# A state-space convolution beside a mixture of experts: totals of scales by way of DRAM, the first block's operands kept, and three changes of order

## The chip, the cores and the metric

The kernel runs on one core of a Trainium2 chip. The time is the device time of one execution in microseconds (us), given as the median of the runs. The core's engines run their own instruction streams in order and wait for each other by semaphores: TensorE (PE in the profile, its weight loads PEld), VectorE (DVE), ScalarE (ACT), GpSimd (POOL) and SyncE (SP). DMAs are issued from SP and POOL in the kernel before.

## The reference, cut to what matters

```python
xn = layernorm(A_u)                              # 2048 tokens, 512 wide
# A: a diagonal state-space kernel K per channel, and a causal convolution
P  = exp(dt * A * l)                             # 512 channels, 128 states, 2048 steps, complex
K  = einsum("dn,dnl,dn->dl", C, P, dt * B).real
y  = irfft(rfft(pad(xn.T)) * rfft(pad(K))) + xn * Dskip
# B: eight experts, all of them chosen for every token
gates = softmax(xn @ w_gate)                     # top 8 of 8
for e in range(8):
    out += gates[:, e] * (silu(xn @ w1[e]) @ w2[e])   # w1 512x1792, w2 1792x512
return x + y + out
```

## The kernel before, in words

**Precision.** Every large product is made from float16 pairs: a float32 operand is scaled by a power of two and split into a high half (ACT: `hilo`'s activation, L442) and a low half (DVE: L445), and a product is three matmuls, high by high, high by low, low by high. The scale of a weight matrix comes from its sum of squares: ACT squares pieces and accumulates per partition (`square`, L438), DVE adds the columns (`prepass_end`, L406), and the total over the 128 partitions is a matmul of a matrix of ones with that one column (`pow2_total`, L160 to L171: the matmul at L170 into a PSUM tile, a copy out by ACT at L165). `pow2_scale` then makes the power of two on DVE. There is such a total for each of `w1[e]` and `w2[e]` (tot_w; expert 0's `w1` has tot_a and tot_b instead), and one for each of the 32 chunks of the state-space part (tot_k).

**Blocks.** Tokens go in four blocks of 512 (tb), and the loops are expert e, block tb, then four groups d of the 1792 hidden columns (seven pairs pr of 256: 2, 2, 2, 1). In every block but the very first, the first product is a Strassen-like scheme of seven half-size products (`block`, `product`, L1307): it needs seven sums and differences of quarters of x in `xop`, and seven of quarters of `w1` in `w1s`. Each group has four slots: products into three PSUM banks A, B, C (tiles hb), with copies of A into B (L1526) and B into C (L1534) and copies out (`keep`, L1521: scC, sE, scB) on ACT. POOL adds sE to scC and scB by accumulating DMAs (L1492); ACT then applies silu (L1323) and makes the high half of the hidden values (L1327: ahl), DVE the low half (L1336). The second product pops finished units of it from a list (`pop`, L1290 to L1292: tiles y, 512 columns). A block's y is scaled by the gate on ACT (`evacuate`, L1266: ye) and accumulated in DRAM.

**Operands of x.** The seven forms of a block's x, high and low, lie in DRAM (`xd`), and the seven slices of `xop` are loaded again for every block (L1517), each in the last group of the block before, as soon as its product is issued. They are made once, during expert 0: `x_sums` normalises two tiles of tokens on DVE and makes the sums, `x_high` (L250) and `x_low` (L257) split them, and `x_turn` transposes them on TensorE (L274, tiles tp), after which ACT copies them out (L285) and SP sends them. The very first block (e = 0, tb = 0) is worked plainly (`plain`, L1572) from `xT0`, all four tiles of x normalised (`xplain`, L296 and L298), split (L304), transposed (`xplain_turn`, L308) and copied into `xT0` (`xplain_out`: tiles 0, 1, 3 by ACT at L315, tile 2 by DVE at L313). `xT0` is not kept: for the seven other experts block 0 is loaded, normalised and transposed a second time, in eight turns, as the last of the blocks.

**The state-space part (s4)** runs in the background beside the experts, 32 chunks of 16 channels: tables on DVE, the kernel K by small matmuls (L729, tile kgen), squares and a copy out by ACT (`s4_kernel_out`: row krow, tile ksb at L737 and L738), a change of layout by way of DRAM (kd at L743, four loads of kt at L745), a scale (`s4_ksplit`: the total tot_k, then `s4_kscale`, `s4_khigh`, `s4_klow`), transforms by matmul (uf, kf, yp) and the convolution itself on DVE (L831, L832).

**What sets the order.** The order of the instructions on each engine is written by hand. A clock counts slots (four per group; the first block has 14). `side`, `mid` and `early` hold work for given slots of expert 0 (`at`, `put`). `work` is a list of items (squares, splits, the ends of a prepass) from which `work_on` takes up to two per slot; `bg_run` lets the s4 generators run as far as a budget of DVE time goes. tp, tot, kgen, uf, kf, yp and the gates' logits share one PSUM bank: `take_bank` hands it on, and a holder that still has to be read is read first (`bank_free`, `bank_wait`).

```python
        st = pow2_total(r, 1, f"w{e}_{w}")        # prepass_end, L408
        yield
        if bank["out"]:
            take_bank()
```

**The start.** `first_square`, `first_split` and `keep_busy` stand in a hand-written row from L1094 on: squares of the first weight pieces, the first scale sA from two of them, fillers on TensorE (L1105), and the splits of the first two pieces. `third` queues the split of the third piece.

**The end.** The last block's four output tiles are made by DVE straight from PSUM onto the loaded sum (L1273), and SP stores each (L1275).

Of the kernel before, what the change touches and what calls it, by code (L numbers as in the profile page):

```python
# [32 lines left out]
def s4_moe_kernel(  # L33
# [59 lines left out]
    xnd = dr.tile([P, NT, D], F32, name="xnd")  # L93
    kds = [dr.tile([P, 4, 64], F32, name=f"kd{n}") for n in range(2)]
# [5 lines left out]
             "act": 0.0, "act0": 0.0, "pe1": 0.0, "actleft": 0.0}  # L100
# [10 lines left out]
    def bank_free():  # L111

        if bank["out"]:
            take_bank()
        return clock["slot"] > bank["at"]
# [56 lines left out]

    def pow2_scale(dst, st, nm, add=0):

        it = sb.tile([P, st.shape[-1]], I32, tag="p2b", name=f"it_{nm}", bufs=2)
        V.tensor_scalar(it, st.bitcast(I32), 24, 23, op0=ALU.logical_shift_right, op1=ALU.logical_shift_left)
        V.tensor_scalar(dst.bitcast(I32), it, -1.0, float((204 + add) << 23), op0=ALU.mult, op1=ALU.add)
# [41 lines left out]
    def x_stats(g):  # L219
        if g:  # L220
            xs_["rs8", g] = norm_stats(g)
        else:
            rs8 = xs_["rs8", 0] = sb.tile([P, TPB], F32, tag="rs8", name="rs8again")
            V.tensor_scalar(rs8, rstd[:, 0:TPB], float(2 ** XSH), None, op0=ALU.mult)
# [65 lines left out]

    xp = {}

    def xplain(j, rs8):

        xn = sb.tile([P, D], F32, tag="fa", name=f"xn{j}")
# [14 lines left out]
    def xplain_out(j):  # L310
        dst = xT0.rearrange("p a k t -> p (a k) t")[:, :, j * P:(j + 1) * P]
        if j == 2:
            V.tensor_copy(dst, xp[j])  # L313
        else:
            S.copy(dst, xp[j])  # L315
# [88 lines left out]
    def prepass_end(e, w, n):  # L404
# [3 lines left out]
        st = pow2_total(r, 1, f"w{e}_{w}")  # L408
        yield
        if bank["out"]:  # L410
            take_bank()
# [46 lines left out]
    def w1_split(e, pr, raw):  # L458

        dst = w1s[pr].rearrange("p a o c -> p a (o c)")  # L460
# [6 lines left out]
    def w2_split(e, pr, raw):  # L467
        return hilo(w2s[pr].rearrange("p a f d -> p a (f d)"), raw.rearrange("p a c -> p (a c)"), scales[e][:, 1:2])
# [30 lines left out]
    def piece_end(e, w, n, ready):  # L499
        st = {}  # L500

        def s0(raw):
            st["g"] = prepass_end(e, w, n)
            step(0)
            clock["dve"] += 0.2

        def step(n):
            st["at"] = now()
            next(st["g"], None)
            done.add((e, w, n))  # L510

        def s1(raw):
            step(1)

        def s2(raw):
            step(2)
            clock["dve"] += 2.5

        def later():
            return now() > st["at"] + 1 and bank_free() and now() + 1 not in turns  # L520
        its = [Item(None, [s0], ready), Item(None, [s1], later), Item(None, [s2], later)]
        for it in its:
            it.e, it.w = e, w
        return its
# [27 lines left out]
    def work_on(limit):  # L552
        while limit > 0:
# [18 lines left out]
            limit -= 1  # L572
            last = not it.steps
# [160 lines left out]
    def s4_kernel_out(c):  # L734
# [8 lines left out]
        nc.sync.dma_start(kd, ksb.rearrange("p j g m -> p j (g m)"))  # L743
        for jh in range(4):
            nc.sync.dma_start(kt[32 * jh:32 * jh + 32].rearrange("x (s g) m -> x s (g m)", s=4),  # L745
                              kd[:, jh, :].rearrange("(s x) c -> x s c", s=4))
        s4["kt", c] = kt

# [216 lines left out]
    def s4_ksplit(c):  # L965

        yield from until(("ke", c))
        yield from bank_wait()
        s4["kst", c] = pow2_total(s4["krow", c], 1, f"k{c}", lambda: s4.update({("read", c): now()}))
        s4["total", c] = now()  # L970
        yield None
        while ("read", c) not in s4:
            bank_free()
            if ("read", c) not in s4:
                yield None
        yield from until(("read", c), more=0)
# [142 lines left out]
    sq(2)  # L1119
    stA = pow2_total(row2[:, 0:1], 1, "a")  # L1120
    take_bank()
    xplain_turn(1)
    keep_busy(8, ident)
# [3 lines left out]
    xplain_out(0)  # L1127
    xplain_turn(2)
    low0 = first_split(0)
    xplain(3, rs8_0)  # L1130
    keep_busy(8, ident)
    xplain_out(1)
    xplain_turn(3)
    xplain_out(2)
    low0()
    xplain_out(3)
    keep_busy(8, ident)
    sq(3)
    sq(4)
    low1 = first_split(1)  # L1140
    sq(5, True)
    sq(6)
    low1()
# [118 lines left out]
    def evacuate(e, i, y):  # L1262
# [9 lines left out]
        else:  # L1272
            V.scalar_tensor_tensor(stg[i], y, g, stg[i], op0=ALU.mult, op1=ALU.add)  # L1273
        if e == E - 1 and i >= NT - TPB:
            nc.sync.dma_start(out[i * P:(i + 1) * P, :], stg[i])  # L1275
# [90 lines left out]
    early, mid = {}, {}  # L1366
# [58 lines left out]
    halves = [(g, a) for g in (2, 3, 0) for a in range(2)]  # L1425
    for n, (g, a) in enumerate(halves):
        s0 = 20 + 4 * n
        at(s0, lambda g=g, a=a: x_high(g, a))
# [9 lines left out]
        if a == 0:  # L1438
            at(s0 + 3, lambda g=g: x_sums(g, 1))
            if g:  # L1440
                at(s0 + 3, lambda g=g: load_x((g + 1) % NB))
        elif g:
            if g + 1 < NB:
                at(s0 + 1, lambda g=g: norm_sums(g + 1))
            at(s0 + 2, lambda g=g: x_stats((g + 1) % NB))
            at(s0 + 3, lambda g=g: x_sums((g + 1) % NB, 0))

    def slot(e, tb, d, s, pops):
# [16 lines left out]
        elif e == 0 and tb == 1:  # L1465
            work_on(2 if d < 3 else 0)
# [27 lines left out]
    def block(e, tb, d):  # L1494
# [32 lines left out]
        clock["act"] += 2 * at_(n * TH)  # L1527
        if later:
            later.pop(0)()
# [31 lines left out]
    def plain():  # L1561

        for f in range(NF):
# [5 lines left out]
            for k in range(KT):  # L1569
                o = ((0, 1), (3, 2))[fh][k // 2]  # L1570
                for (a, b) in ((0, 0), (0, 1), (1, 0)):
                    T.matmul(h, w1s[pr][:, a, o, k % 2 * P:(k % 2 + 1) * P], xT0[:, b, k, :],  # L1572
                             start=(n == 0), stop=(n == 3 * KT - 1))
                    n += 1
# [5 lines left out]
            if f == 1:  # L1580
                activate(0, 0, 0, hb[0], 0, 0, True, high)
            activate(0, 0, pr, hb[f % 3], fh, 0, True, high)
            for g in high:
                g()
            if f == 1:
                third()
# [76 lines left out]
```

## Time and profile before

| what | value |
| --- | --- |
| median of 3 runs | 2345.7 us (2345.11 to 2345.76) |
| the profiled execution's own time | 2344.99 us |
| its span | 2343.2 us |
| TensorE busy | 2324.7 us, 17818 matmuls |
| DVE busy | 1964.2 us |
| ACT busy | 1473.5 us |
| POOL busy | 339.6 us |
| DMA moved | 319.68 MB |

Rows of the timeline read: start in us from the span's start, duration, engine, line of the kernel, operation, out<-in, shapes, count; in brackets how long the engine idled before and what ended that. Rows of groups end with busy time, the mean duration in ns, and the idle time before them. Several instructions in a row of one kind are merged into one row, with the count after x. A matmul's duration contains its way through the array, so matmuls of one stream overlap; the distance between two starts is what one costs the stream.

### The profile page before, as it was taken

Reading aid. Unit: us, or ns where it says so; the run is one execution under the profiler, and the core shown is the slowest. Engines: PE = TensorE matmul, PEld = TensorE weight load, DVE = VectorE, ACT = ScalarE, POOL = GpSimd, SP = SyncE. Lnnn points to the kernel's source line nnn. Section 1 sums busy time; section 2 is a strip of 40 time slices with the busy share of each in tenths; the row PEclk is TensorE's granted clock in tenths of the full one; section 3 lists DMA queues with packets and bytes.
Section 4 is the critical chain, followed back from the end, with each engine's and each line's share of the span. In section 5 each row is a group of like instructions: output and inputs, shape, how many; then the busy total and the mean of one; then the engine's idle time right before and its main releaser. Section 6 shows DMA issues by size and latency. Waiting matters only on the chain.

```text
span 2343.2 us, 45501 instructions
## 1 busy us (share of the span) xinstructions
PE 2324.7 (99%) x17818; PEld 1552.8 (66%) x17818; DVE 1964.2 (84%) x3814; ACT 1473.5 (63%) x2596; POOL 339.6 (14%) x394
## 2 busy tenths in 40 slices
PE   8999999999999999999999999999999999999999
PEld 4567666666666666666666666666666666666665
DVE  7864878889898899998899989998899988997721
ACT  7586667556665566665666657666576665765543
POOL 0011001121111211101111111111111110111112
PEclk9999999999999999999999999999999999999999
DMA  7586555774667746654556455565465654643456
GB/s 252 167 254 145 144 156 148 163 158 95 139 143 165 155 102 138 154 130 102 115 127 166 120 105 122 132 151 121 103 147 117 150 124 95 150 89 69 83 114 149
DMA packets 330503, 319.68 MB, mean 136 GB/s; under 512 B 190832, under 2 KB 223088, under 8 KB 329968
## 3 DMA queue, kind: packets, MB, share of 16 engines
q1 hardware_dynamic: 274416, 223.17, 32.4%
q0 software_dynamic: 55872, 93.61, 25.3%
q8 instruction: 139, 2.28, 0.4%
q14 instruction: 76, 0.62, 0.1%
HBM read 202.14 MB, written 65.01 MB: 114 GB/s over the span
## 4 chain that ended last, share of the span: by engine, by line
PE 94%; ACT 2%; issue 2%; DVE 1%; DMA 1%; SPq 0%; DVEq 0%; ACTq 0%; POOLq 0%
PE hb L1307 42%; PE y L1291 16%; PE y L1292 16%; PE y L1290 16%; PE kgen L729 1%; PE yp L860 1%; PE kf L800 1%; PE uf L787 1%; DMA scC<-sE 0%; PE tp L274 0%; ACT ahl L1327 0%; ACT fa L1323 0%; ACT w1s L442 0%; PE hb L1572 0%; DMA raw<-in_w_dram 0%
## 5 line engine op out<-in xcount | busy, mean ns | idle before, releaser
L1307 PE MATMUL hb<-xop,w1s 128*128 128x256 f16 x9114 | 1072.8, 273 | 3.3 <-ACT scC L1521 2.0
L1307 PEld LDWEIGHTS <-w1s 128*128 128x128 f16 x9114 | 889.0, 98 | 171.7 <-issue 5.1
L1290 PE MATMUL y<-w2s,ahl 128*128 128x512 f16 x1792 | 679.2, 379 | 0.9 <-ACT ye L1266 0.9
L1292 PE MATMUL y<-w2s,ahl 128*128 128x512 f16 x1792 | 679.2, 379 | 0.0
L1291 PE MATMUL y<-w2s,ahl 128*128 128x512 f16 x1792 | 679.2, 379 | 0.0
L1292 PEld LDWEIGHTS <-ahl 128*128 128x128 f16 x1792 | 175.3, 98 | 211.4
L1492 POOL DMA_DIRECT2D scC<-sE x124 | 117.6, 948 | 1295.0 <-ACT sE L1521 1095.0
L1323 ACT ACTIVATE fa<-hb,sc 128x512 f32<-128x512 f32 (+1 forms) x252 | 160.3, 636 | 199.4 <-PE hb L1307 198.9
L1291 PEld LDWEIGHTS <-ahl 128*128 128x128 f16 x1792 | 175.3, 98 | 162.2 <-issue 1.2
L832 DVE TENSOR_TENSOR s<-s,tm 128x720 f32<-128x720 f32 (+14 forms) x480 | 268.9, 560 | 16.6
L1290 PEld LDWEIGHTS <-ahl 128*128 128x128 f16 x1792 | 175.3, 98 | 161.1
L831 DVE TENSOR_TENSOR tm<-v,k 128x720 f32<-128x720 f32 (+14 forms) x480 | 267.3, 557 | 10.3
L1336 DVE SCALAR_TENSOR_TENSOR ahl<-fa,sc,ahl 128x512 f16<-128x512 f32 (+1 forms) x262 | 178.7, 682 | 57.6 <-ACT ahl L1327 57.3
L1534 ACT COPY hb<-hb 128x512 f32<-128x512 f32 x124 | 64.2, 518 | 240.5 <-PE hb L1307 240.3
L1327 ACT ACTIVATE ahl<-fa,sc 128x512 f16<-128x512 f32 (+1 forms) x262 | 175.8, 671 | 8.5
L1526 ACT COPY hb<-hb 128x512 f32<-128x512 f32 x124 | 64.3, 518 | 176.2 <-PE hb L1307 175.4
L1492 POOL DMA_DIRECT2D scB<-sE x124 | 107.5, 867 | 426.8 <-ACT scB L1521 287.6
L1336 DVE SCALAR_TENSOR_TENSOR ahl<-scB,sc,ahl 128x512 f16<-128x512 f32 x124 | 84.4, 681 | 77.4 <-ACT ahl L1327 74.1
L717 DVE TENSOR_TENSOR tb<-ta,tt 128x64 f32<-128x64 f32 (+2 forms) x192 | 132.0, 687 | 5.7
L711 DVE TENSOR_TENSOR ta<-tb,zr 128x64 f32<-128x64 f32 (+2 forms) x192 | 131.6, 686 | 5.3
L1269 POOL DMA_DIRECT2D oacc<-ye x108 | 95.9, 1339 | 252.8 <-ACT ye L1266 251.1
L714 DVE TENSOR_TENSOR tt<-tb,zi 128x64 f32<-128x64 f32 (+2 forms) x192 | 130.4, 679 | 0.0
(245 smaller groups left out, 2444.6 us busy)
## 6 DMA issues: line engine op xcount, KB each, us to landing
xop<-xd SPq DMA_DIRECT2D x210, 256.0 KB, 4.0
pp<-in_w_dram SPq DMA_DIRECT2D x98, 512.0 KB, 4.2
raw<-in_w_dram SPq DMA_DIRECT2D x56, 512.0 KB, 4.8
oacc<-ye POOLq DMA_DIRECT2D x108, 256.0 KB, 6.2
scC<-sE POOLq DMA_DIRECT2D x93, 256.0 KB, 4.2
scB<-sE POOLq DMA_DIRECT2D x93, 256.0 KB, 3.9
raw<-in_w_dram SPq DMA_DIRECT2D x52, 256.0 KB, 3.4
raw<-in_w_dram SPq DMA_DIRECT2D x104, 128.0 KB, 3.8
```

The source lines that it names most:

```text
L711: V.tensor_tensor(ta, tin, zrv, op=ALU.mult)
L717: V.tensor_tensor(tout, ta, tt, op=ALU.add)
L831: V.tensor_tensor(tm, v3f[:, :, 0:n], kb, op=ALU.mult)
L832: V.tensor_tensor(s3[:, :, m:], s3[:, :, m:], tm, op=ALU.add)
L1290: T.matmul(y, lhs[0], w2s[pr][:, 0, fh, :], start=(c == 0), stop=False)
L1291: T.matmul(y, lhs[0], w2s[pr][:, 1, fh, :], start=False, stop=False)
L1292: T.matmul(y, lhs[1], w2s[pr][:, 0, fh, :], start=False, stop=(c == NF - 1))
L1307: T.matmul(dst[:, q, :], w1s[pr][:, a, wo, k * P:(k + 1) * P], xop[:, xo, b, k, :], start=(first_mm and q == 0 and n == 0), stop=(n == 5), ...
L1323: S.activation(fa, src[:, :n], AF.Silu, scale=w1_unscale(e, d if whole else prs[0]))
L1327: S.activation(ahl[:, 0, :n], fa, AF.Copy, scale=scales[e][:, 3:4])
L1336: V.scalar_tensor_tensor(ahl[:, 1, :n], fa, sc[:, 3:4], ahl[:, 0, :n], op0=ALU.mult, op1=ALU.subtract)
L1492: nc.gpsimd.dma_start(dst, src, accum_op=ALU.add)
```

## The change

**Totals.** Three new helpers take the place of `pow2_total` for every expert but the first and for all s4 chunks: the column of 128 partial sums is stored to DRAM (`total_send`), loaded back so that each partition holds all 128 (`total_fetch`), and summed along the row by ACT (`total_sum`). In `prepass_end` the steps lie at least two slots apart; in the s4 part the column is sent just behind kd, fetched behind the kt loads, and summed two slots after the chunk's `s4_kernel_out`.

```diff
+    def total_send(row, nm):
+        rd = dr.tile([P, 1], F32, name=f"rd_{nm}")
+        nc.sync.dma_start(rd, row)
+        return rd
+    def total_fetch(rd, nm):
+        bt = sb.tile([P, P], F32, tag="bt", name=f"bt_{nm}", bufs=1)
+        nc.sync.dma_start(bt, rd.rearrange("p a -> (p a)").partition_broadcast(P))
+        return bt
+    def total_sum(bt, nm):
+        st = sb.tile([P, 1], F32, tag="p2a", name=f"st_{nm}", bufs=2)
+        S.activation(bt, bt, AF.Copy, accum_out=st)
+        clock["act"] += at_(P) + 0.2
+        return st
...
     def s4_ksplit(c):
         yield from until(("ke", c))
-        yield from bank_wait()
-        s4["kst", c] = pow2_total(s4["krow", c], 1, f"k{c}", lambda: s4.update({("read", c): now()}))
-        s4["total", c] = now()
+        s4["kst", c] = total_sum(s4["kbt", c], f"k{c}")
```

`piece_end` becomes one item of five steps instead of three items, and no longer asks for the bank. `bank_free` refuses the bank in a slot of which `work_on` took two items.

**Block 0's operands.** The normalised tiles of the start are kept (tag hh) and stored; the three of the seven forms that are plain quarters go from `xT0` to `xd[0]` in slots 8 to 10, and `xT0` as a whole to `x0d` in slot 11. In place of the second pass `xT0` is loaded again (slot 31), and the other four forms are made from what is already transposed.

```diff
+    def x0_send(n):
+        if n < 4:
+            nc.sync.dma_start(xnd[:, n, :], xp["xn", n])
+        elif n < 7:
+            k, t = ((0, 0), (2, 0), (2, TH))[n - 4]
+            for b in range(2):
+                nc.sync.dma_start(xd[0][:, n - 4, b], xT0[:, b, k:k + 2, t:t + TH])
+        else:
+            nc.sync.dma_start(x0d, xT0)
...
-    halves = [(g, a) for g in (2, 3, 0) for a in range(2)]
+    halves = [(g, a) for g in (2, 3) for a in range(2)]
...
+    for k in range(2):
+        at(35 + 3 * k, lambda k=k: x0_sums(k))
+        at(36 + 3 * k, lambda k=k: x0_high(k))
+        at(37 + 3 * k, lambda k=k: x0_low(k))
```

`x0_sums` makes the four forms on DVE in five instructions for each of two k, `x0_high` and `x0_low` split them; there is no transpose and no copy out of PSUM.

**Order of the first block.** Of the four copies into `xT0` ACT now makes tiles 0 and 1 and DVE tiles 2 and 3; the square of the third piece moves behind the first split, that of the fourth from ACT to DVE; and the matmuls of `plain` take the eight with the high weights first and the four with the low ones last. `third` is called before the second activation instead of behind it.

```diff
-                for (a, b) in ((0, 0), (0, 1), (1, 0)):
+            ops = [(k, 0, b) for k in range(KT) for b in range(2)] + [(k, 1, 0) for k in range(KT)]
+            for k, a, b in ops:
```

**Order of the second block** (e = 0, tb = 1). The first `x_high` of block 2 is issued behind the copy of A into B of group 1, ahead of the activations that follow there, and `work_on` takes fewer items from group 2 on:

```diff
+        for f in copied.get((e, tb, d, 0), ()):
+            f()
         if later:
             later.pop(0)()
...
-            work_on(2 if d < 3 else 0)
+            work_on(2 if (d, s) < (2, 1) else 1 if (d, s) == (2, 1) else 0)
```

**The last output** is made and stored in two halves of 256 columns, one by SP and one by ACT:

```diff
-            V.scalar_tensor_tensor(stg[i], y, g, stg[i], op0=ALU.mult, op1=ALU.add)
-        if e == E - 1 and i >= NT - TPB:
-            nc.sync.dma_start(out[i * P:(i + 1) * P, :], stg[i])
+            for h, q in ((0, nc.sync), (1, nc.scalar)):
+                c = slice(h * TH, (h + 1) * TH)
+                V.scalar_tensor_tensor(stg[i][:, c], y[:, c], g, stg[i][:, c], op0=ALU.mult, op1=ALU.add)
+                q.dma_start(out[i * P:(i + 1) * P, c], stg[i][:, c])
```

149 lines of the change are left out of this document (87 added, 62 removed).

## The prediction, made before the changed kernel had run

> **What bounds the kernel now.** I read the page first, then who waited for whom on TensorE, then TensorE's groups by shape, then the timeline at the places where it waited.
>
> ```profile
> span 2343.2 us, 45501 instructions
> PE 2324.7 (99%) x17818; PEld 1552.8 (66%) x17818; DVE 1964.2 (84%) x3814; ACT 1473.5 (63%) x2596; POOL 339.6 (14%) x394
> ```
>
> TensorE is busy 99% of the span. A busy TensorE need not be at its peak, so I look at starts. In this stretch of an ordinary block the matmuls of 512 columns follow each other at 0.22 us (0.216 over a longer run: the 26 at 23.95, quoted further down, fill 5.77, so (5.77 - 0.38) / 25):
>
> ```profile
> 386.77 0.38 PE L1291 MATMUL y<-w2s,ahl 128*128 128x512 f16 x1
> 386.99 0.38 PE L1292 MATMUL y<-w2s,ahl 128*128 128x512 f16 x1
> 387.21 0.28 PE L170 MATMUL tot_k<-krow,ones 128*128 128x1 f32 x2
> 387.35 0.49 PE L1307 MATMUL hb<-xop,w1s 128*128 128x256 f16 x3
> ```
>
> The y matmul before the total starts 0.22 before it, as it does before another y; the next product starts 0.14 after it. So one total (two passes) costs TensorE **0.14 us**, whatever its listed duration of 0.28. That matters because there is little else to gain: TensorE's waits are few.
>
> ```profile
> PE tp L308 <- ACT xhl L298: 6.6, 1, 6.6
> PE hb L1307 <- ACT scC L1521: 2.0, 3, 0.9
> PE y L1290 <- ACT ye L1266: 0.9, 1, 0.9
> ```
>
> The longest, 6.6, is the wait for the first inputs and is not touched. The other two come after 100 us and are waits for ScalarE (ACT); the rest of the view (two waits for ACT in the second block, shown below, and some of 1.4 us or less in the first 31 us) is no longer. A gain can only come from taking instructions off TensorE, or from these waits and the first 30 us. The matmul work itself (products and y) is the same in both kernels.
>
> **The change part by part.**
>
> *Totals by way of DRAM and the transposes of the first block.*
>
> ```profile
> L170 PE MATMUL tot_k<-krow,ones 128*128 128x1 f32 x64 | 8.9, 208 | 0.0
> L170 PE MATMUL tot_w<-r,ones 128*128 128x1 f32 x30 | 4.2, 208 | 0.0
> 115.57 0.61 PE L274 MATMUL tp<-ident,xh 128*128 128x128 f16 x8
> 116.02 0.38 PE L1290 MATMUL y<-w2s,ahl 128*128 128x512 f16 x1
> ```
>
> The 64 records of tot_k are 32 totals, the 30 of tot_w are 15; one of the latter stays (expert 0's). 46 x 0.14 = **6.4 us** off TensorE. Eight transposes take from 115.57 to 116.02, 0.056 each; block 0's second pass, two halves of 28 by the slices in x_turn, 56 in all, goes: **3.1 us**. Nothing on TensorE replaces either. ACT loses 46 copies of a total and eight copies out of PSUM, and gains 46 sums of 128 columns with a read of the accumulator; it is busy 63%, so I cost the exchange at nothing apart from its waits, below. DVE's work for block 0 is about the same. SP's queue gets some 100 DMAs more; behind them stand the loads of the next block's operands:
>
> ```profile
> SPq L1517 <- PE hb L1307: 291.4, 118, 61.3
> ```
>
> SP waits 291.4 us for TensorE ahead of these loads, 2.5 each, because it is early; 100 more issues near 0.42 (row below) are 42 us in all. So nothing is late, and I cost the issues at nothing; without that lead a load behind two of them would come 0.8 late.
>
> *Order of the first block.* Rows of the start, in order of time:
>
> ```profile
> 13.20 0.62 ACT L298 CAST xhl<-xn 128x512 f16<-128x512 f32 x1
> 13.65 1.06 PE L1105 MATMUL hb<-ident 128*128 128x128 f16 x8
> 13.73 1.00 ACT L315 COPY tb<-tp 128x1024 f16<-128x1024 f16 x1
> 16.32 0.69 DVE L304 TENSOR_TENSOR xhl<-xn,xhl 128x512 f16<-128x512 f32 x1 [1.32 <-ACT xhl L298]
> 16.93 0.68 DVE L313 COPY tb<-tp 128x1024 f16<-128x1024 f16 x1
> 17.30 0.61 PE L1105 MATMUL hb<-ident 128*128 128x128 f16 x8
> 17.53 1.28 DVE L445 SCALAR_TENSOR_TENSOR w1s<-raw,sA,w1s 128x1024 f16<-128x1024 f32 x1
> 18.57 1.67 PE L1572 MATMUL hb<-tb,w1s 128*128 128x512 f16 x7 [0.65 <-ACT tb L315]
> 23.95 5.77 PE L1572 MATMUL hb<-tb,w1s 128*128 128x512 f16 x26
> 30.12 4.92 PE L1572 MATMUL hb<-tb,w1s 128*128 128x512 f16 x22 [0.40 <-DVE w1s L445]
> ```
>
> The first product waits for the fourth copy of transposed x, which ACT makes last. In the new order ACT does, from 13.20: copy of tile 0 (1.00), casts of tiles 2 and 3 (0.62 each), done by 15.4. DVE follows each cast with a low part of 0.69, done near 16.1; the last transposes end near 17.05; DVE copies tile 3 in 0.68 and ends near 17.8. Products start near 17.85 instead of 18.57. They now take the eight matmuls with the high weights first, 8 x 0.216 = 1.73, and DVE's low part (1.28, behind the copy) is ready by 19.1, in time. Of the 0.7 a little is lost again at the second total, which needs all squares: DVE's queue up to it (17.8, two low parts of 1.28, four squares near 0.65) ends near 23.1, so I keep 0.55. The 26 matmuls from 23.95 reach 23.95 + 26 x 0.216 = 29.57, and the next starts at 30.12: a hole of 0.55 for weight tile 2, whose high half ACT now makes before the second activation, and whose low half comes last in the group. It goes. **1.1 us** for the start.
>
> *Order of the second block.*
>
> ```profile
> 103.84 0.42 DVE L241 TENSOR_TENSOR xfb<-xfa,xfb 128x256 f32<-128x256 f32 x1
> 108.12 0.72 ACT L1323 ACTIVATE scC<-scC,sA 128x512 f32<-128x512 f32 x1 [4.42 <-DMA scC<-sE]
> 110.64 1.04 ACT L250 CAST xh<-xfa 128x1024 f16<-128x1024 f32 x1
> 111.30 0.38 PE L1292 MATMUL y<-w2s,ahl 128*128 128x512 f16 x1
> 112.31 0.59 ACT L1534 COPY hb<-hb 128x512 f32<-128x512 f32 x1
> 112.95 0.27 PE L1307 MATMUL hb<-xop,w1s 128*128 128x256 f16 x1 [1.27 <-ACT hb L1534]
> 117.72 0.58 ACT L1521 COPY scC<-hb 128x512 f32<-128x512 f32 x1
> 118.35 0.27 PE L1307 MATMUL hb<-xop,w1s 128*128 128x256 f16 x1 [0.87 <-ACT scC L1521]
> 136.46 1.04 ACT L438 ACTIVATE pp<-pp 128x1024 f32<-128x1024 f32 x1
> 138.53 0.50 PE L274 MATMUL tp<-ident,xh 128*128 128x128 f16 x6 [0.70 <-ACT xs L285]
> ```
>
> ACT idles 4.42 before 108.12 for a DMA, and then makes two casts (110.64 to 112.31) ahead of the copy that TensorE needs. Their inputs are there at 104.3 (DVE, 103.84 + 0.42), so put ahead of the wait they fit into the idle time. The copy then ends near 111.2, before TensorE asks at 111.30 + 0.216: a hole of 112.95 - 111.52 = 1.43 goes. ACT runs on without a break to the copy at 117.72, now near 116.1, ending 116.65; TensorE, itself 1.43 earlier, asks near 115.9. That wait shrinks only from 1.03 to about 0.75. The wait before 138.53 (0.86 beyond the pitch) stands behind a square at 136.46 that moves to the next block; it goes. Together **2.5 us**. The wait on ye (0.9) hangs on the DMA at 108.12 and stays.
>
> *Last output in halves, on two queues.*
>
> ```profile
> 2337.14 2.73 DVE L1273 SCALAR_TENSOR_TENSOR fin<-y,gse,fin 128x512 f32<-128x512 f32 x4 [9.73 <-PE y L1292]
> ```
>
> DVE's four end at 2339.87, and the last store can leave then. Two halves cost one instruction more on DVE, but half of the last tile's bytes leave some 0.35 earlier, half of its 2.73 / 4. No row shows an issue by ACT; bounds -0.3 to +0.3, I take a gain of **0.2**.
>
> *What is added: ACT waits for a load.* The squares' row goes to DRAM and comes back spread over the partitions, 64 KB.
>
> ```profile
> DMA to landing us min/median/max: 1.7/3.2/8.5
> kt<-kd SPq DMA_DIRECT2D x128, 32.0 KB, 1.9
> L745 SPq DMA_DIRECT2D kt<-kd x128: 318/424/1872, 327.8 to 2156.9; - x128
> L1526 ACT COPY hb<-hb 128x512 f32<-128x512 f32 x124 | 64.3, 518 | 176.2 <-PE hb L1307 175.4
>   PE tot_w L170: 10.6, 5
> ```
>
> The first row is the kd store's (128 KB), from the view of the tile ksb. In an s4 chunk the new load stands on SP behind that store and the four kt loads, which were there before: 3.2, then five issues of 0.42 (the median in the L745 row), then the landing, between 1.9 (32 KB) and 3.2 (128 KB), I take 2.5: 7.7 us. ACT asks two slots after. A block is 7 x 7 x 6 products of 256 columns at half the y spacing, 0.108, and 28 x 6 y matmuls at 0.216, 68.0 us in 16 slots, so two slots are 8.5 us on average, and 5.2 in the last group of a block (per slot 12 products and six y matmuls). There ACT can be held some 2.5 us. Behind it stand the next block's copy of B and the activations; ACT idles 176.2 / 124 = 1.4 us before each such copy because it is early, and in the first group of a block TensorE has three y units (3.9 us) and a product to do before it needs that copy. The narrow waits fall at the end of a block, just ahead of this wide place. The trace has a like case: ACT waited 10.6 us, five times 2.1, for a weight total, and no TensorE wait stands beside these. I cost the waits at **0.5 us**; bounds 0 and ten narrow waits (so many chunks' sums fall there by the program's slots) x 2.5 = 25 us if nothing hid them. By the Trainium skill (SBUF — State Buffer, its fit of 2 us plus bytes over 436 GB/s) the 64 KB would land after 2.15 us, an estimate; the chain would be 7.4 us and the sum unchanged.
>
> The new order also deals anew the few places where ACT has a copy for TensorE behind other work (the other two of the three scC waits); I leave them at 0.1 worse, -1.5 to +1.5.
>
> Sum: 6.4 + 3.1 + 1.1 + 2.5 + 0.2 - 0.5 - 0.1 = 12.7. The profiled execution took 2344.99 (span 2343.2 and 1.8 around it): 2332.3. The median of the runs, 2345.7, lies 0.7 above that execution, so I forecast **2333.0**.
>
> **The rivals.**
>
> *More collisions.* With the bank no longer held for totals, the s4 steps come earlier and meet the weight splits at the ends of experts. One such meeting costs about 1 us (the 0.9 in the scC row); four to six more give 2337 to 2339. For it: ACT's queue is in order. Against: only two in some 2200 us before. 0.12.
>
> *The wait on ye goes as well.* If the shifted start lets the scC load of the second block land earlier relative to TensorE, up to 1.05 and the rest of the 0.75 go: 2331. 0.10.
>
> *DVE is the real pace.* It is busy 84%; if freed TensorE time is eaten by waits for DVE, only the start, the second block and the tail (3.8) stay: 2342. Against: after the first 31 us no wait of TensorE names DVE. 0.06. This is also how it would look if the change did not do what it says.
>
> *Slow clock at the start.* Eight fillers take 1.06 at 13.65 and 0.61 at 17.30, so the spacing halves in between. If the moved order delays that and the first eight products still run at twice 0.216, they cost 8 x 0.216 = 1.7 more: 2334.7. Against: TensorE's own order at the start is the same. 0.04. The Trainium skill has the rule for this (TensorE: Matmul & The Clock Gate, Part 1: a gate sets the clock by the activity in a window of about 3.4 us); by its figure one window at half speed also costs 1.7, an estimate.
>
> *Slower: the load comes late everywhere.* If the stores typically land like the slowest kd store, 8.5 us instead of 3.2, the chain is 13 us, ACT is held 13 - 8.5 = 4.5 us at 46 places, 3.1 of it beyond its 1.4 of lead: 143 us, 2475.
>
> It decides from 0.4 us of uncovered wait per total (46 x 0.4 = 18.4 against 12.7 + 4.7), that is a typical chain of 10.3 us, 2.6 more than I take; just there the time is 2351. By the Trainium skill (DMA: Bandwidth & Descriptors, Specifications) writes under 512 B become read-modify-writes, which speaks for it: the row is 128 pieces of 4 bytes. No row here shows that price. Against: the row's store runs beside the kd store, on which SP waits anyway. 0.04.
>
> **How the numbers follow.** Forecast 0.64 (2330 to 2336.5 by its own bounds), collisions 0.12, ye 0.10, DVE 0.06, clock 0.04, slower 0.04. Below 0.2% (4.7 us) a measurement of this kernel cannot be told from no change, so faster means under 2341.0. Faster: 0.64 + 0.12 + 0.10 + 0.04 = 0.90; DVE falls within: 0.06; slower 0.04. The range 2329.5 to 2339 takes in the forecast, the ye case, the clock and the collisions, and leaves out the last 0.10 and the bounds' tails.
>
> **What would show it.** Right: TensorE has 92 records of tot and 56 of tp fewer; the first product of L1572's successor starts near 17.9 and no hole stands before the fifth group; the wait on the C copy near 111 us is gone; ACT waits on bt are a few us each in the last group of blocks and no TensorE wait follows them. Wrong: TensorE waits on the hb copies with ACT held by bt before them (the slower case), waits that name DVE (the pace), or a total of TensorE waits after 140 us above 5 us (collisions).

## The result, and the profile after

The changed kernel takes **2496.56 us** (median of 4 runs, 2488.24 to 2500.71) against 2345.73 beside it: ratio **1.064** (95%: 1.0625 to 1.0651), 163.6 us over the forecast of 2333.0. The page of the profiled execution, its span, TensorE's row and the two rows of the chain:

```profile
span 2494.7 us, 45325 instructions
...
PE 2357.3 (94%) x17670; PEld 1555.5 (62%) x17670; DVE 1968.5 (79%) x3816; ACT 1475.3 (59%) x2631; POOL 340.4 (14%) x394
...
PE 65%; DMA 17%; ACT 7%; DVE 6%; issue 3%; SPq 2%; POOL 0%; DVEq 0%; ACTq 0%; POOLq 0%
PE hb L1365 31%; PE y L1348 10%; PE y L1349 10%; PE y L1350 10%; DMA bt_k<-rd_k 6%; DMA rd_k<-krow 5%; DMA kd<-ksb 4%; SPq L807 1%; ACT ahl L1385 1%; PE kgen L790 1%; DMA base<-in_u_dram 1%; DVE ahl L1394 1%; PE yp L923 1%; DVE tm L894 1%; ACT fa L1381 1%
```

TensorE has the 148 records fewer that were forecast (17818 to 17670). Yet it idles 2494.7 - 2357.3 = 137.4 us where it idled 18.5, and it is busy 32.6 us longer with less to do. 118.9 + 32.6 is the whole 151.5 us of the span. The chain, 94% TensorE before, now runs for 15% through three DMAs of the s4 chunks. Who waited for whom, on TensorE and then on ACT (us in total, times, longest):

```profile
PE hb L1365 <- ACT hb L1589: 60.1, 14, 8.1
PE hb L1365 <- ACT hb L1599: 31.5, 10, 6.0
PE hb L1365 <- ACT scC L1584: 26.8, 9, 9.2
```

```profile
ACT bt_k L192 <- DMA bt_k<-rd_k: 215.5, 32, 13.5
```

ACT waits for the spread row of every one of the 32 chunks, 6.7 us each, and TensorE waits 118.4 us for three kinds of copies that ACT, which works in order, makes behind that sum. Of the 14 weight totals there is next to nothing (5.5 us of ACT):

```profile
ACT bt_w L192 <- DMA bt_w<-rd_w: 5.5, 5, 2.4
```

The view of the DMAs, with the size of each and the median from issue to landing:

```profile
xop<-xd SPq DMA_DIRECT2D x210, 256.0 KB, 4.7
...
kd<-ksb SPq DMA_DIRECT2D x32, 128.0 KB, 7.9
kt<-kd SPq DMA_DIRECT2D x128, 32.0 KB, 6.1
...
bt_k<-rd_k SPq DMA_DIRECT2D x32, 64.0 KB, 5.1
...
rd_k<-krow SPq DMA_DIRECT2D x32, 0.5 KB, 8.7
```

The smallest of these transfers, 0.5 KB, is the slowest. The kd store next to it took 3.2 us before and takes 7.9, kt 1.9 and now 6.1, xop 4.0 and now 4.7. (Such a median rests on the issues whose landing the trace tells, for kd 12 of 32. The starts in the timeline cover all 32 chunks: from kd's issue to the first kt load, which waits for kd to land, 3.3 us before and 6.7 now, medians.) One chunk, in the timeline (start, us, engine, line; in brackets the idle time and what ended it):

```profile
818.99 0.37 ACT L799 COPY ksb<-kgen 128x256 f32<-128x256 f32 x1
...
825.77 0.38 SPq L804 DMA_DIRECT2D kd<-ksb  x1
...
826.19 0.43 SPq L180 DMA_DIRECT2D rd_k<-krow  x1
...
829.30 0.60 ACT L853 ACTIVATE upad<-uf 128x512 f32<-128x512 f32 x1
...
834.31 0.82 PE L863 MATMUL kf<-kh,dfth 128*128 128x256 f16 x6
836.36 1.74 SPq L807 DMA_DIRECT2D kt<-kd  x4
838.20 0.38 SPq L186 DMA_DIRECT2D bt_k<-rd_k  x1
...
843.35 0.31 ACT L192 ACTIVATE bt_k<-bt_k 128x128 f32<-128x128 f32 x1 [13.46 <-DMA bt_k<-rd_k]
...
843.66 0.57 ACT L1584 COPY scC<-hb 128x512 f32<-128x512 f32 x1
...
844.28 2.93 PE L1365 MATMUL hb<-xop,w1s 128*128 128x256 f16 x13 [9.15 <-ACT scC L1584]
```

This is one of the worst chunks. kd was issued late, at 825.77, 6.4 us after ksb was copied. The kt loads could go only at 836.36, 10.6 us behind it, and the spread load stands behind them. ACT, in order, stands still from 829.9 to 843.35, TensorE from 835.1 to 844.28. Over all 32 chunks, by the starts in the timeline (means): kd is issued 0.5 us after ksb is copied, the spread load 10.3 us after kd, and the sum starts 4.9 us after that, 15.8 in all. ACT is ready for it after 9.0, hence the 6.7 us each.

The 13 matmuls of 256 columns behind the hole take 2.93 us, twice the usual 0.109 each: the clock is down (the granted clock averages 0.978 over this run, 1.000 before). By the starts of all matmuls after 25 us there are 41 such holes, 131.2 us, and 35.7 us more in 317 matmuls at twice their pitch, the usual distance of two starts (before: 8 holes, 6.5 us, and 0.5). All 15 holes of 3.58 us or more are followed by matmuls at the slow pitch that lose 1.2 to 2.6 us, the 18 under 2.5 us by 0.2 at most; of the eight between, four are. The Trainium skill (TensorE: Matmul & The Clock Gate, HAM oscillation — how this bites in real kernels) says that an idle gap of about 3.4 us halves the rate of what follows. This trace agrees for the longer holes; that half of those between 2.5 and 3.58 us did it too is more than that figure says.

The other parts of the change are where they were forecast. The start and the second block, from the timeline:

```profile
17.92 5.34 PE L1637 MATMUL hb<-tb,w1s 128*128 128x512 f16 x24 [0.34 <-DVE tb L375]
...
23.33 10.52 PE L1637 MATMUL hb<-tb,w1s 128*128 128x512 f16 x48
...
108.82 0.38 PE L1348 MATMUL y<-w2s,ahl 128*128 128x512 f16 x1 [0.82 <-ACT ye L1323]
...
110.11 2.78 PE L1365 MATMUL hb<-xop,w1s 128*128 128x256 f16 x24
...
115.28 1.91 PE L1365 MATMUL hb<-xop,w1s 128*128 128x256 f16 x16 [0.65 <-ACT scC L1584]
...
134.60 0.50 PE L293 MATMUL tp<-ident,xh 128*128 128x128 f16 x6
```

The first product starts at 17.92 (forecast 17.85), and 48 matmuls run without a hole from 23.33 (10.52 = 47 x 0.216 + 0.38). TensorE no longer waits for the copy into C (before: 1.27 us ahead of 112.95; now the product at 110.11 follows without a wait), and the transposes of block 2 start at 134.60 instead of 138.53: 3.9 us ahead, forecast 1.1 + 2.5.

### The profile page after: what moved, and what is told of

It is laid out like the page before. It is cut to its first block, busy times and chain, and to the rows that moved or that the text cites. A ratio compares the mean times of both kernels' runs of the same rounds, so it can differ in the third digit from the quotient of the medians.

```text
span 2494.7 us, 45325 instructions
## 1 busy us (share of the span) xinstructions
PE 2357.3 (94%) x17670; PEld 1555.5 (62%) x17670; DVE 1968.5 (79%) x3816; ACT 1475.3 (59%) x2631; POOL 340.4 (14%) x394
## 4 chain that ended last, share of the span: by engine, by line
PE 65%; DMA 17%; ACT 7%; DVE 6%; issue 3%; SPq 2%; POOL 0%; DVEq 0%; ACTq 0%; POOLq 0%
PE hb L1365 31%; PE y L1348 10%; PE y L1349 10%; PE y L1350 10%; DMA bt_k<-rd_k 6%; DMA rd_k<-krow 5%; DMA kd<-ksb 4%; SPq L807 1%; ACT ahl L1385 1%; PE kgen L790 1%; DMA base<-in_u_dram 1%; DVE ahl L1394 1%; PE yp L923 1%; DVE tm L894 1%; ACT fa L1381 1%
## 5 line engine op out<-in xcount | busy, mean ns | idle before, releaser
L1365 PE MATMUL hb<-xop,w1s 128*128 128x256 f16 x9114 | 1103.8, 277 | 121.5 <-ACT hb L1589 60.1
L1365 PEld LDWEIGHTS <-w1s 128*128 128x128 f16 x9114 | 903.6, 99 | 321.6 <-issue 123.0
L1394 DVE SCALAR_TENSOR_TENSOR ahl<-scC,sc,ahl 128x512 f16<-128x512 f32 x124 | 84.4, 681 | 98.8 <-ACT ahl L1385 98.8
L192 ACT ACTIVATE bt_k<-bt_k 128x128 f32<-128x128 f32 x32 | 9.9, 309 | 215.5 <-DMA bt_k<-rd_k 215.5
```

The lines of the kernel that those rows point to most:

```text
L1365: T.matmul(dst[:, q, :], w1s[pr][:, a, wo, k * P:(k + 1) * P], xop[:, xo, b, k, :], start=(first_mm and q == 0 and n == 0), stop=(n == 5), ...
L1394: V.scalar_tensor_tensor(ahl[:, 1, :n], fa, sc[:, 3:4], ahl[:, 0, :n], op0=ALU.mult, op1=ALU.subtract)
```

## The experiments

Two theories at first. **Theory 1**: ACT reaches the chunk's sum before its row is in, and everything else follows from that. **Theory 2**: the stores of 4 bytes per partition slow all other transfers, and ACT's place in line is secondary. "The kernel with the chunks' totals by matmul" is the changed kernel with the old code for the 32 chunks. Times are medians; the kernel before took 2345.6 to 2345.9 beside all of them.

**All totals by matmul again** (`prepass_end`, `piece_end`, `s4_kernel_out` and `s4_ksplit` as before the change):

```diff
-            rd = total_send(r, f"w{e}_{w}")
...
+        st = pow2_total(r, 1, f"w{e}_{w}")
...
-        s4["kst", c] = total_sum(s4["kbt", c], f"k{c}")
+        s4["kst", c] = pow2_total(s4["krow", c], 1, f"k{c}", lambda: s4.update({("read", c): now()}))
```

> The changed kernel with all 46 totals by the ones matmul again; the transposed x, the ordering of the first two blocks and the halved last output stay. Theory 1 (the added 151 us all belong to the chunks' totals: ACT reaches the sum before its row is in) and theory 2 (the 4-byte stores slow every transfer, ACT's place in line is secondary) both give the three terms read off the changed kernel's trace without the totals: 3.1 us for 56 transposes, 1.3 at the start and 2.6 in the second block to the good, 0.2 at the tail to the bad: 2345.7 - 6.8 = 2338.9 us, 2337 to 2341. If another part of the change were to blame (x0d's loads, the order of the second block), it stays above 2345.7.

Measured 2364.95: 26 us over both theories. Its timeline has one hole that the changed kernel does not have, ahead of the last block:

```profile
2249.79 0.81 PE L926 MATMUL yp<-zh,dfth 128*128 128x256 f16 x6 [0.67 <-ACT k L869]
2270.12 0.63 ACT L912 ACTIVATE zh<-z 128x512 f16<-128x512 f32 x1 [20.38 <-DVE z L906]
...
2271.16 1.22 PE L926 MATMUL yp<-zh,dfth 128*128 128x256 f16 x5 [20.56 <-ACT ysb L933]
```

TensorE has nothing left but the s4 work, which the plan must finish before the last block (`bg_until`). In this mixture the plan ends it at slot 503; before the change it was 494. This is tested further down.

**Only the chunks' totals by matmul** (the `s4_` lines of the diff above alone):

> Only the 32 chunks' totals by matmul again; the 14 totals of the other experts' weights stay by way of DRAM. Theory 1: they have slots to spare (ACT waited 2.4 us in all for them), so each saves a ones matmul of 0.14 us: the kernel without any DRAM totals less 14 x 0.14 = 2.0, about 2337. Theory 2: 14 of the 46 stores remain, so 14/46 of the 151 us remain, some 2385; in part, some us above the kernel without any.

Measured 2336.22 (ratio 0.9962, 0.9947 to 0.9977). The weights' stores cost nothing that shows; the whole loss lies in the chunks' totals. Theory 2 does not hold for the 14 stores of the weights.

**The sum five slots later**, the weights' totals by matmul:

```diff
-        yield from until(("ke", c))
+        yield from until(("ke", c), more=4)
         s4["kst", c] = total_sum(s4["kbt", c], f"k{c}")
-        yield None
-        yield None
```

> The 32 chunks' totals by way of DRAM as in the change, but ACT's sum is given out 5 slots (about 23 us) after the store instead of 2, and the two empty slots behind it are taken out; the weights' totals by matmul. The chain it has to cover was 14.7 us. Theory 1: the sum finds its row in, the holes go, and the 32 ones matmuls saved show: the kernel without any DRAM totals less 32 x 0.14 = 4.5, about 2334.5, up to 2341 if the later end of the chunks' work costs a wait at the end. Theory 2: stores and loads are all there, kd's landing stays near 7.9 us, kt's near 6.1 and xop's near 4.7, and it stays over 2360.

Measured 2369.58. The number meets theory 2 (over 2360, with kd at 6.4, kt at 5.0 and xop at 4.5), but the step down speaks for theory 1: 127 us, most of the loss, are gone with ACT's early sum. Some 30 us are not (against 2339.08, a kernel with all totals by matmul that comes further down), and TensorE's waits have another name:

```profile
PE hb L1368 <- DMA xop<-xd: 19.7, 6, 7.1
```

**A store that nobody waits for**, added to the kernel with the chunks' totals by matmul:

```diff
         nc.sync.dma_start(kd, ksb.rearrange("p j g m -> p j (g m)"))
+        rd = total_send(row, f"k{c}")
```

> The kernel with the chunks' totals by matmul, but each chunk's row is also stored to DRAM behind kd, and nobody loads it or waits for it. It does the reference's work and 32 stores more. Theory 1: a store that nobody waits for is beside the work, within 2 us of the kernel without it (about 2337 to 2339). Theory 2: the 128 pieces of 4 bytes hold the queues, kd's and kt's landings go from 3.2 and 1.9 us toward 7.9 and 6.1, and the time goes up by 10 us or more.

Measured 2379.3, 43.1 us more for 32 stores of 512 bytes. So both theories hold in part. (At 1.35 us a store, the weights' 14 would cost 19; they don't. Behind a chunk's store SP waits for kd at once, behind a weight's it does not; that this is the difference was not tried.) The DMA view of this run, and then the landing row of its kd store (min, median, max):

```profile
kt<-kd SPq DMA_DIRECT2D x128, 32.0 KB, 5.5
...
rd_k<-krow SPq DMA_DIRECT2D x32, 0.5 KB, 9.5
```

```profile
DMA to landing us min/median/max: 1.7/4.2/14.8
```

The store lands after 9.5 us though nobody reads it. kt takes 5.5 (1.8 without the store), kd in the worst case 14.8. The medians of kd, 4.2 here and 4.1 without the store, rest on 10 and 18 of 32 landings and hide the difference: by the starts of all 32 chunks it is 6.9 us from kd to the first kt load here and 3.1 without the store. The next four runs ask what is slow about it.

**The same 4 bytes 512 bytes apart**:

```diff
+        rd = dr.tile([P, P], F32, name=f"rd_k{c}")
+        nc.sync.dma_start(rd[:, 0:1], row)
```

> The kernel with the unread store, but each partition's 4 bytes go to a place of their own, 512 bytes apart. The unread store cost 43.1 us (2379.3 against 2336.2). Theory A (the 128 pieces get in each other's way in one stretch of 512 bytes): the stores land like kd's, 3 to 4 us, and the time falls to 2336 to 2342. Theory B (a write of less than a whole stretch is slow wherever it goes): landing stays near 9.5 us and the time near 2379. Theory C (one more transfer of 128 pieces on SP's queue ahead of kt): stays near 2379 with a short landing.

**512 bytes of each partition** (values of ksb, read by nobody):

```diff
+        rd = dr.tile([P, P], F32, name=f"rd_k{c}")
+        nc.sync.dma_start(rd, ksb.rearrange("p j g m -> p (j g m)")[:, 0:P])
```

> The kernel with the unread store, but 128 pieces of 512 bytes (64 KB of ksb's values in place of the row, to a tensor that nobody reads). Theories A and B: whole stretches, so it lands in 3 to 4 us and the time is 2336 to 2342 although 128 times as many bytes move. Theory C: near 2379.

**The loads alone** (one row, stored in chunk 0, spread in every chunk behind kt):

```diff
+        if c == 0:
+            s4["rd"] = total_send(row, f"k{c}")
...
         s4["kt", c] = kt
+        total_fetch(s4["rd"], f"k{c}")
```

> The kernel with the chunks' totals by matmul and, behind each chunk's kt, a load of 64 KB that gives every partition the same 512 bytes from a row stored once (chunk 0), read by nobody. It measures the load of the change without its stores and without ACT's wait. If the load is harmless (both theories, so far): 2336 to 2340, landing near 5 us. If 128 readers of one stretch hold the queues as the stores do: kt and xop land later and the time goes up by 10 us or more.

Measured 2338.06, 2337.85 and 2339.81. Theory A holds: as many pieces as small cost 1.8 us instead of 43.1 when each has a place of its own, and 128 times the bytes cost 1.6; neither is clear of the spread of the runs. From kd to the first kt load it is 3.3 and 3.1 us again. Theories B and C are out. The loads cost 3.6. Nothing was tried between pieces side by side and pieces 512 bytes apart, so how large the shared stretch is stays open. In the run with the places apart, the DMA view:

```profile
kd<-ksb SPq DMA_DIRECT2D x32, 128.0 KB, 3.0
kt<-kd SPq DMA_DIRECT2D x128, 32.0 KB, 1.8
...
rd_k<-krow SPq DMA_DIRECT2D x32, 0.5 KB, 3.1
```

**The forms by themselves**, one after the other, without the reference's work:

```diff
+        near = dr.tile([P, 1], F32, name=f"near{r}")
+        nc.sync.dma_start(near, src[:, 0:1])
...
+        apart = dr.tile([P, P], F32, name=f"apart{r}")
+        nc.sync.dma_start(apart[:, 0:1], src[:, 0:1])
```

> None of the reference's work: six forms of transfer one after the other, 8 times, each waiting for the one before, with nothing beside them: 4 bytes of each partition to one stretch of 512 bytes (near), the same 512 bytes apart (apart), 512 bytes of each partition (wide), 1 KB of each partition (kd), 4 bytes of each partition into one partition's row on chip and from there in one piece to DRAM (row, one), and near with a kd right behind it (both, behind). Theory A: near lands in 8 to 9 us here too, apart, wide and kd in 2 to 3, and behind in 7 or more. Theory B: near and apart both at 8 to 9. If near lands in 2 to 3 us alone, the 8.7 us came from the other traffic and not from the form.

The first of its eight passes in the timeline (354.3 us in all, one run); each issue waits for the landing of the one that it reads, so distances of starts are landings:

```profile
3.26 0.33 SPq L29 DMA_DIRECT2D near<-src  x1
10.30 0.33 SPq L31 DMA_DIRECT2D bcast<-near  x1
15.47 0.16 DVE L25 TENSOR_TENSOR src<-src,bcast 128x1 f32<-128x1 f32 x1 [12.24 <-DMA bcast<-near]
15.66 0.32 SPq L35 DMA_DIRECT2D apart<-src  x1
17.09 0.32 SPq L37 DMA_DIRECT2D backa<-apart  x1
...
22.55 0.32 SPq L47 DMA_DIRECT2D kd<-src  x1
24.26 0.32 SPq L49 DMA_DIRECT2D backk<-kd  x1
...
26.58 0.54 SPq L53 DMA_DIRECT2D row<-src  x1
28.52 0.30 SPq L55 DMA_DIRECT2D one<-row  x1
29.63 0.34 SPq L57 DMA_DIRECT2D bcone<-one  x1
32.53 0.16 DVE L25 TENSOR_TENSOR src<-src,bcone 128x1 f32<-128x1 f32 x1 [5.98 <-DMA bcone<-one]
...
33.09 0.43 SPq L63 DMA_DIRECT2D behind<-src  x1
...
42.91 0.32 SPq L65 DMA_DIRECT2D backb<-behind  x1
```

With nothing beside it, the store into one stretch of 512 bytes takes 7.0 us (7.0 to 7.7 in the eight passes), the same pieces apart 1.4, kd's form 1.7. The same kd right behind such a store takes 9.8 (9.2 to 10.5). By way of one partition's line on chip the row is spread after 1.9 + 1.1 + 2.9 = 5.9 us instead of 7.0 + 5.2 (the 5.2 is the longest of eight, 4.2 the shortest). By the profile the DMA engines are done with it early: the store is issued at 3.26, their busy share is 0.19 from 4.0 to 4.4 and 0.00 from 4.4 to 10.3. The rest is waiting until the landing is reported; why that takes so long, no run shows. That gives a test that changes the form of the store and keeps the order of the work.

**The row by way of a line on chip**, at the changed kernel's own places (`ones` is free by then and serves as the line and as the buffer of the spread row):

```diff
-        rd = total_send(row, f"k{c}")
+        nc.sync.dma_start(ones[0:1, :], row)
+        rd = dr.tile([1, P], F32, name=f"rd_k{c}")
+        nc.sync.dma_start(rd, ones[0:1, :])
...
-        s4["kbt", c] = total_fetch(rd, f"k{c}")
+        nc.sync.dma_start(ones, rd.rearrange("a p -> (a p)").partition_broadcast(P))
```

> The changed kernel in its own order, sum two slots after the row, but the chunk's 128 sums go by another way: 4 bytes of each partition into one partition's line on chip, from there to DRAM in one piece of 512 bytes, then the same load. Alone these three took 1.9, 1.1 and 2.9 us, 5.9 in all, against 7.0 and 5.2. If the form of the store is the cause of the 151 us: the chain is 8 to 10 us here, ACT waits a few us in some chunks, and the time is 2332 to 2350. If the place of the sum in ACT's order is a cause of its own, also with a quick row: over 2400.

**The same with the sum four slots after the row** (`more=3`, the two empty slots taken out):

> As the run with the line on chip, and the sum given out four slots after the row, without the two empty slots behind it. Both causes are away, so the prediction's terms should show: 2336.2 (chunks' totals by matmul) less 32 ones matmuls x 0.14 = 4.5: 2331.7, 2330 to 2336. If transfers on SP's queue cost something of themselves (the unread loads cost 3.6), 2336 to 2340.

**The change's own store with that later sum** (`rd = total_send(...)`, loaded into `ones`):

> The change's own store and load, with the sum given out four slots after the row, as in the run with the line on chip and the later sum; only the form of the store differs from that one. If the wait of ACT and the slowed transfers are two separate costs: some 35 to 43 us over the run with the line on chip, 2365 to 2377, with kd near 6 us and TensorE waiting for xop. If the wait was all: within 5 us of it.

Measured 2363.99, 2349.86 and 2383.3. None of the three lies where it was expected: the first is between its two cases, so that both causes count; the second is 10 us over the higher of its ranges; the third is 33.4 us over the second, near the 35 to 43 of two separate costs, but above 2377 because the second is. With the changed kernel's 2496.56 they make a table of two by two, by the form of the store and the place of the sum. (Two things change along: the row is spread into `ones` in all but the changed kernel, where SP hardly waits for the buffer, 2.6 us, and the later place goes without the two empty slots.)

| | sum two slots after | sum four slots after |
|---|---|---|
| 4 bytes into one stretch | 2496.6 | 2383.3 |
| line on chip, one piece | 2364.0 | 2349.9 |

The form alone is worth 132.6 us, the place alone 113.3, both together 146.7. Either mends most of it, since the long landing hurts most through ACT's wait. ACT's wait for the chunks' rows, in the waits of the run with the line and its own place, and of the run with the slow store and the later place:

```profile
ACT ones L192 <- DMA ones<-rd_k: 62.6, 16, 8.1
```

```profile
ACT ones L192 <- DMA ones<-rd_k: 11.5, 7, 3.0
```

215.5 falls to 62.6 and 11.5. In the second of the two the loss is elsewhere: TensorE waits 12.4 us in 7 places for xop, which comes late:

```profile
PE hb L1363 <- DMA xop<-xd: 12.4, 7, 3.9
```

But 2349.9 was to be 2331.7.

**The plan of the first run in time**: one empty slot per chunk fewer in the kernel with all totals by matmul, so that the s4 work ends at slot 494:

```diff
         s4_khigh(c)
         yield None
-        yield None
         s4_klow(c)
```

> The kernel with all totals by matmul took 2365.0 where 2338.9 was expected; its trace has one hole of 20.7 us at 2250 us, ahead of the last block, where the chunks' work ends at slot 503 of the plan instead of 494. Here one empty slot of each chunk is taken out, so that the plan ends at slot 494 again. If the late end of the plan is the cause: 2365.0 - 20.7 = 2344.3, 2338 to 2345. If it is something in the totals by matmul themselves: stays over 2355.

Measured 2339.08 (ratio 0.9973, 0.9962 to 0.9983), and the hole of 20.6 us is gone. The late end of the plan was the cause; the hole itself is 20.6 of the 25.9 us that went. 2339.08 is also what the terms of the prediction give for everything but the totals (2345.88 beside it, less 6.8).

**SP not standing still for the row**: the piece to DRAM behind kt, the load two slots after the row.

```diff
-        yield from until(("ke", c), more=3)
+        yield from until(("ke", c), more=1)
+        nc.sync.dma_start(ones, s4["rd", c].rearrange("a p -> (a p)").partition_broadcast(P))
+        yield from until(("ke", c), more=3)
```

> As the run with the line on chip and the later sum (2349.9, 18 us over what was expected of it), but SP's queue never stands still for the row: the piece to DRAM is issued behind kt, and the load two slots after the row, two slots ahead of the sum. If SP's standing still for the row (97.8 us in 32 waits there) is what cost the 18 us: 2331 to 2336. If the 4-byte pieces into one line slow the transfers beside them: it stays at 2344 to 2352.

**The row into the line, read by nobody**, in the kernel with the chunks' totals by matmul:

```diff
+        line = sb.tile([P, P], F32, tag="bt", name=f"line_k{c}", bufs=1)
+        nc.sync.dma_start(line[0:1, :], row)
```

> The kernel with the chunks' totals by matmul, and each chunk's row also sent 4 bytes at a time into one partition's line on chip, which nobody reads. If this form is harmless, as the stores 512 bytes apart were (2338.1): 2336 to 2339. If 128 pieces of 4 bytes into one line get in each other's way as in DRAM, though less (1.9 us alone against 7.0): kd and kt land later and the time is 2345 or more.

Measured 2344.5 (2341.67 to 2348.14) and 2337.74. By its number alone the former would speak for slow pieces; the latter speaks against that (1.5 us over the kernel without the row, within the spread). SP's standing still accounts for 5.4 of the 18 us. Some 13 us stay. The trace of the former has 11 holes, 13.5 us together, the longest 4.1 at 797 us, and the waits behind them name ACT at different copies:

```profile
PE hb L1366 <- ACT scC L1585: 4.6, 2, 3.9
PE hb L1366 <- ACT hb L1590: 3.8, 3, 1.4
```

In this kernel the plan ends the s4 work at slot 487, seven slots early (in its trace the last transform starts 117.9 us before the end of the span, 91.0 before the change), so that more of it may fall together with the weights' work on ACT. That this is the cause was not tested and stays open.

**The last output whole**, in the kernel with the chunks' totals by matmul:

> The kernel with the chunks' totals by matmul (2336.2), with the last block's output computed and stored whole, as before the change. The changed kernel's last output to the end of the span took 4.75 us against 4.57 before, so 0.2 to 0.5 less, about 2336.0; no difference that a run can tell is expected. Over 2337.5 the halves would have been worth something after all.

Measured 2335.99, 0.2 less than in halves, which a run can't tell apart. With the output whole or in halves this is the best version found: the weights' totals by DRAM, the kept transposed x and the new order, the chunks' totals by matmul. Whole, its ratio to the kernel before is **0.9959** (0.9945 to 0.9972).

## Why the prediction was wrong

- **The step that failed: "What is added: ACT waits for a load".** It took the row's store at the landing of the kd store, 3.2 us, and the load at 2.5, and reached 7.7 us (its terms add up to 7.8) against two slots of 8.5. Two slots were right: ACT comes 9.0 us after ksb. The chain was not: the load is issued 10.3 us after kd, where 3.2 and four issues of 0.42 made 4.9, and its sum starts another 4.9 us later, where 0.42 and 2.5 made 2.9. The runs show a landing of 8.7 for the row's store, and with nothing beside it still 7.0; of 5.1 for the load. The mistake was the nearest row: kd's pieces are 1 KB and have places of their own, the row's are 4 bytes and share one stretch. The bounds (0 to 25 us) came from the same row and could not hold a miss of 163.6.
- **"Against: the row's store runs beside the kd store, on which SP waits anyway"** was wrong in kind. The row's store does not hide behind kd, it delays kd, although kd is issued first: from kd to the first kt load 3.3 us before, 6.7 in the changed kernel, 6.9 with the store unread. (With nothing else running 1.7 became 9.8, but there kd was issued behind the store.) SP, in order, stands still for kd's landing 153.3 us in all instead of 105.5, and 74.8 us for the row's. That SP is otherwise early, on which the prediction costed the issues at nothing, does not help here. Behind kd, the kt loads, xop and the issue of the spread load go late; unread, the stores still cost 43.1 us.
- **The slower rival was the mechanism**, with a chance of 0.04. Its price, 143 us, came from 3.1 us of uncovered wait at 46 places; in the trace it is 118.4 us behind 32 chunks, and 35.7 us of halved clock, most of it behind the long holes, which it did not count. That the two sums lie near each other, 143 and 154, is partly chance. The rule cited there from the Trainium skill (DMA: Bandwidth & Descriptors, Specifications: writes under 512 B become read-modify-writes) pointed the right way, but the size of a piece alone does not set the price: pieces of 4 bytes 512 bytes apart landed after 1.4 us alone and 3.1 in company, as whole ones did (1.5 and 3.1). What costs is that many lie side by side. Whether a read-modify-write is what makes these wait for each other, no run shows.
- **Lead of ACT.** That narrow waits fall ahead of wide places was fair for the weights' totals (5.5 us of ACT in all), and of no help against 6.7 us in every chunk.
- **The rest of the sum was right, to the tenth by luck.** Without any DRAM totals 2339.08 was measured, 6.8 us under before; the terms were 3.1 + 1.1 + 2.5 + 0.2 - 0.1 = 6.8. In parts: start 1.3, up to the second block's end 3.9 in all, so 0.3 more than forecast; the 3.1 of the transposes was not measured apart. The tail was the wrong way round: from the last y matmul's start to the end of the span 4.57 before, 4.79 after, as DVE's eight halves take 3.23 us where four whole ones took 2.73.
- **Totals, 0.14 each.** The 14 weight totals, 2.0 us by the prediction, measure 2.9 (2339.08 to 2336.22, two medians whose ranges overlap; the former's plan also has a slot per chunk fewer). The 4.5 us of the chunks' totals were not obtained in any run.
- **Collisions** (four to six more, when the bank is no longer held) may be part of the 13 us left open once the store is out of the way; that was not shown.

## What to carry to other kernels

Before costing a new transfer at a neighbour's landing, compare where its pieces go, not only how many bytes they are: 128 pieces of 4 bytes into one stretch of 512 bytes took 7.0 to 9.5 us and held up what came behind. A queue that works in order turns the landing into a wait for all that stands behind the reader, so ask what the row costs if it is 10 us late. When totals, loads or steps are taken out of a planned schedule, look where the plan now ends: one kernel here lost 25.9 us to nothing else, 20.6 of them in one hole.

## What the runs showed of the hardware that was not expected

- A store of 128 x 4 bytes, with nothing beside it: 7.0 to 7.7 us into one stretch of 512 bytes, 1.4 into places 512 bytes apart, 1.9 into one partition's line on chip. A kd store of 128 KB right behind the first: 9.2 to 10.5 instead of 1.7. The profile shows the DMA engines idle for most of that time (share 0.00 from 4.4 to 10.3 us of the first).
- The load that spreads 512 bytes to 128 partitions took 4.2 to 5.2 us when the row had just been stored in 4-byte pieces and 2.9 to 3.1 when it had been stored in one. In the kernel, from a row stored long ago, its median was 3.8, in the changed kernel 5.1. Why the first is slower was not tried.
